# Angles of three gate groups summed by TensorE with a triangle of ones instead of scans, the state products' second weights 32 columns wide, and a new order of the tasks

## The chip, the cores and the metric

The kernel runs on one core of one Trainium2 chip. The metric is the device time of one execution in microseconds (us). Of the kernel before there are three timed runs: 762.91, 760.21 and 762.88 us, with a median of 762.88. The profile shown is of one more execution, which took 765.08 us; its span from the first to the last recorded instruction is 763.4 us, so 1.7 us lie around the span. The mean granted TensorE clock of that execution is 0.998.

## What is computed

Two blocks follow each other. The first is a linear attention with a complex gate, for 4 batches, 8 heads, 768 tokens and a head dimension D of 48; the second is an MLP on its output, with 3072 tokens, a model dimension of 384 and 2048 hidden features. Cut to what matters:

```python
mag = np.sqrt(a_re * a_re + a_im * a_im)
scale = np.minimum(mag, 0.999) / (mag + 1e-06)
a_re_n, a_im_n = (a_re * scale, a_im * scale)
for t in range(S):
    new_re = ar * S_re - ai * S_im
    new_im = ar * S_im + ai * S_re
    kv = np.einsum('bhd,bhe->bhde', k[:, :, t], v[:, :, t])
    S_re, S_im = (new_re + kv, new_im)
    y[:, :, t] = np.einsum('bhd,bhde->bhe', q[:, :, t], S_re)
...
h = x @ w_in
g = np.maximum(h, 0.0) + alpha * np.minimum(h, 0.0)
return (g @ w_out).astype(np.float32)
```

Each gate is a complex number. A product of gates over tokens has the product of their magnitudes and the sum of their angles, so the kernel needs the running sum of the angles over the tokens of a batch, taken modulo a full turn, and its sine and cosine.

## The kernel before, in words

**Tasks and their order.** Every stage is a Python generator (`gates`, `loads`, `half_rows`, `loads_v`, `pieces`, `weights`, `unit`, `loads_x`, `all_mlp`) that emits one operation, or a few, each time it is resumed. The long string `ORDER` names by a letter which task is resumed next, so it fixes the order of the instructions on every engine and of the loads on SyncE's queue (SP). The `yield DVE(...)`, `yield PE(...)` and so on, and the rings in `R`, carry the costs and buffers of a planner that found the string; here they do nothing. An engine runs its instructions in the string's order, and a waiting instruction holds back everything behind it on its engine.

**Gates.** `gates` runs for nine groups: (batch 0, chunks 0), (0, 1 and 2), (0, 3 to 5), then two groups of three chunks for each further batch. A chunk is 128 tokens (P). A tile holds 128 rows of (head, dimension), with NK = 3 such row blocks side by side, so a group of three chunks is 128x1152. The angles are made on ScalarE (the arctangent, L289), summed along the tokens by one `tensor_tensor_scan` on VectorE for each row block (L298), brought to whole turns by ScalarE (L312, which rounds) and VectorE (L315, which subtracts the whole turns), and handed to the next group of the batch in `carry` (L318). Then come sine and cosine (L328, L330, L333) and the two stores of the phases to `phs` in DRAM (L324). The magnitudes go through L340 to L358 into `decs` (L361). Both are loaded again in another layout, as `PP` (L507) and `T` (L514), by the 24 units.

**Units.** A unit is one chunk of one batch with all 8 heads. It turns q and k by the phases (L579, L581), and passes six levels: copies of q and k (L660, L676), products with the decays in place (L637), small TensorE products `ps_lv` (L596, 96 rows and 32 columns of weights), masks (L610, L620). Then k is transposed by TensorE (`ps_kt`, L708), copied into `T` by two ScalarE copies, and multiplied with v for the state: `ps_kv`, L720, whose weights are slices of `T` of 64 rows and 64 columns. Only 96 of the two times 64 columns are of use, since D2 = 2 * 48 = 96; the second copy, L711, puts the first 32 columns once more behind the 96 so that there is something to load. The states follow on VectorE (L728, L731), and the output `ps_y` by L746 (96 rows, 48 columns of weights) and L760 (64 rows, 48 columns). It is copied (L771), stored to `ysc` (L776) and loaded as `xT`.

```python
nc.scalar.copy(T[:, 4 * i:4 * (i + 1), 0:D2], t)
nc.scalar.copy(T[:, 4 * i:4 * (i + 1), D2:P], t[:, :, 0:P - D2])
...
for n in range(H):
    for j in range(0, P, HC):
        for s in range(1 if last else 2):
```

There s is one half (64 tokens, so 64 rows) of the chunk, j one half of the columns, and a batch's last chunk (`last`) needs only s = 0. In the program each of these matmuls carries the part of the 128x128 array that it uses: 128x32 at L596, 128x64 at L746, 64x64 at L720 and L760, 128x128 at the rest.

**MLP.** `all_mlp` interleaves blocks of two units (256 tokens). The first two blocks go the plain way (L817, then L867), the others by L839 and by seven products of a Strassen scheme (L957). The weights come as 64-bit floats and are made into 32-bit floats piece by piece: `to_f32` uses ScalarE (L435, L437, L439) and VectorE (L443, L445).

**Queues.** All bulk loads and stores are issued by SP, in the order of the string. GpSimd makes the masks at the start.

Of the kernel before, what the change touches and what calls it, by code (L numbers as in the profile page):

```python
# [9 lines left out]
F32 = mybir.dt.float32  # L10
# [4 lines left out]
AF = mybir.ActivationFunctionType  # L15
ALU = mybir.AluOpType
# [3 lines left out]
P = 128  # L20
# [5 lines left out]
TURN = 6.283185307179586  # L26
# [1 line left out]


ORDER = (  # L30
    "ABMABAAABABAAAAAAABMAAAAAMAAAABABBBJMMNMAAAJABBAAKAAAKJJAAAAAAAABBBABJABBBBBBNMBNPBBBPNPJBJKJKJBJBBB"
    "PNBBBPBBBBBBBBBPPPOOOOJLJCPJJLLKKCPOJLLLMLLLLLLLMLLJJOPOPOPNOPPPPONNPPQCPPPQNQCCCCPPPPPPPPPPQQPQPCNC"
    "CCPPPPPPPPPCQQNCCCCCONCCCQOQCNPCPQQQOJMMJPPLMLLJCNQQNORCJLnLCMLLJJJLCCCLLLLQCQRCRQQCCOQNQQQoooooooLL"
    "LNQQRRQNooQQCCCCCNCooQoOoQRQoCQORCCNRRoNooooooORoQOMJONQQoooooRNNOOQQQQRQQROQOQDQQJLRLLnLJJORoLLoooo"
    "LLDMLRNNoLLLLLLooooJDooDDRoooSoSoRRRRRRRRooooooooDRRoRRoRooooRNNNRDSDoDRoDRDSOooooooooRoDoDRSSRJJJJR"
    "RSNSSRRRRDoooooDSDTOooODSLRRoSSoLMLLMJLJLLLLLooSoDSoOTSNoooooSNoOooSSoSoSNSSSSoSDooToSoSooSTSNoooOOo"
    "oNMLLLLLTTSoTSTDSOoTTSDoooooDoDSOKTNoNNNOSSSTSSTSJJJMJLSDDoooooSoooooDJLSSLoOToNTToooToOoOOoooooTTOT"
    "TToTDDTToooooUTnTTooLLLJJLJLDLLLUooooTDToDDoooLLLoLKDoJJJToTTUooDDoDDDTDJTDDDoooooUoTTUTUTTUUUUoVooo"
    "oooooUoTUUVUTTTTVooooooooUUUEJJLLLJJELLLLLLLLLJoLLooooVoEooooUUoUUUEoEVooooooEoEoUVUoUUUoooooUooooEU"
    "UVVUUVUVVVEEEooooooooVoUoKEUVKVUUUUJKKEUUUUKJJJVEVVooVooooEoooEEooEooVVVooooVVVVVVoWoWooooooVoVooJLL"  # L40
    "LJnWooVooVWoLLLLVWWEVEVEEEWEVWWLLLLLLLLEVWWVJEJoKJoooooooooooVVVWVWVVVELKVVLLLLJLJJLLLJJWoWWEWoooooo"
    "oooXXooEEEoEEoooooooooooooooooWWWWWWWoooWXoEWLLLoEoooooooooooWWooooWWoooXoXWWEEEWEEWoJLLLJoooWXWWWEW"
    "XWWWXYWXLWWLLFYXJLnLJJLoooooooXooooooooooooooXXXXXXoooooFoooooooXXFXXoXXXoXooooooooXoXoXYYooooLLLLLL"
    "LLooXXYYXooXYXYYLYooooXooooXFYFooooooXXXXYXYXFYoFYXXXLXLJLJJJLJLLLFooooooooYYoJooooooooooFoooooYYYFF"
    "YooYYooYYoJJLLLJLLJLoZoYooZooYooooFFoooFoYooYYFZoooFFLLooooooooooZooooZZYZYZYFZZYFYFYoooFZYYYZYZYYFo"
    "YooFFYooooooooooFFLLYJJJLooZooooooZZoooooooooooLnFLLFLJLLLJFooLJLLLLZaaFooooooZZoooZFaoFFZZoooooooaF"
    "FoZZZoZFFFoooooooZoooZooaaoooZoZoZZaaZFFFooFJJaoaaZooooooooooooZZZaZZZaZZaoooooooZaoaooabooooooooooo"
    "oooaaooabbZLLZLGJJLLJLJLLGLLLLLaaaoaaooaGooaoooooooJoboaoooaGoobGabaaaJJabbaLKKKoGbGoooooooooooobbbo"
    "ooGGooooGGooooboooooooooababaaGbaGGbGabaLaooooooooocoobLLJJGnKLoooooooooLoLLooobbooocbLLLLLJbbGGGoob"
    "ocooooooLLLKboboboooGGoboooocboooooobbccboocbGbGooooooocccGGoobboooobbbbooooooooooooGcGGKJGGGobcbcbo"  # L50
    "ocbJLJbbLLLJJLocccoooooooooooGooooccGcccocccGdGcoooooooooooocococoocooccoooGGGGcJLLLLLLLLLLdGcocGcoo"
    "oooooodoodooocccddcJJJcdcooooooooooooooooddLLccLHLcJJJLLLJLLdoLdHLLnoooooooodKLLLdddoddooooooooooooo"
    "ooddodddddooHeddoooeodooooodedoHdoooooooooooededdddeeoHddHooooooooeHeeoooHoooddoooooooooooooooddoeee"
    "oddoKJJJJddLLLJeJLLLJJJJLLLeoeoooooooooeHooooHooooooooooffHHooooeeeLJJLLLLLooooooHHHHHHHfooeeooeeeeo"
    "oooooeeoooooooooeoeoooeeeoeHHHfoHeHgefeoooooeeefeHeeKHooofofeeoJJHffoooooooonofHLJLLLLLLLHHooooooooo"
    "offfgoLLJLJJJLLLoofffooooooogHoLooooffoofHHfooooHHHoooooooooofffffoofoofoogoHooooHooooffooooofHHfffH"
    "ffHohhogooooooffgffgffofofhfgogooooooooooooooooggIJJLLLLLLLLJJJIJJgLLLLLLggIgoggIooooooIooooooooooog"
    "goghgIoggogoghIoogooooooogooIoogoogoghhgIhgghIhgoIooohhoooooooooioooooooohogIoIoghggghghhgIggLLLLJJn"
    "hhoooooooooooiLLLLLJLLLLLLJJooohhIhIhhIoooohhhIIihooooooooihoooooooooooooiIhooooooooooooooooooohhJoo"
    "oiiiihhohihIIIohihoooooooJhhihhihihLoohIIiooooooooooiihooooooooooooooiioihILLLoooIiiiijJJLLLJJLLLJji"  # L60
    "iJLLLLLIoiooiooiIiooioiIjiioIIIIIoIooooooooooIIIoiIoooooojiijijiijJIojjjjoooooooooooooooooooijjjjiio"
    "oiijJnJJJLLLLJLLojooooooooooooooooojjjjjjjkkjooooooooojjooojookooooooojoojoookookjkoooookkoooooooooo"
    "oojJJLLLLLLLLLjjoooooookoooooooooojookoooooookooojjjjkjkjjjkLjjkooooooooolkkoLLJJJJJooooookkkokkkook"
    "kooookokkooooolloookooklkllkkkkkloooollooooooooooolJLLLLLLLLLLJLLooooooooooloooooooooklkklkkkklkkLLL"
    "LLnlllooLLLJJLLooooooooooooooollolllloolllooooooolooolmmolloLLLLLoooooloooololmmlooooooooooolooooooo"
    "olmlmlmomomooooooooomoooooooooomoooolmlmlmooooomLLLLLLmomoooooooooLLLLoooooommoooommllmmmmmllLLLLooo"
    "oommoooooomooomooommmmmmmmmomooooooooooommmoooooooooooonoooooooooooooooooooooooooooooooooooooooooooo"
    "oooooooooooooooooooooooooooooooooooooooooooooooooooooooooooooooooooooooooooooooooooooooooooooooooooo"
    "oooooooooooooooooooooooooooooooooooooooooooooooooooooooooooooooooooooooooooooooooooooooooooooooo")


class Ring:
# [25 lines left out]
def kernel(  # L98
# [32 lines left out]
    nc = tc.nc  # L131
    B, HP, _, D, S = q.shape
    H = 2 * HP
    DM, DF = w_in.shape
    NCH = S // P
    NK = DM // P
    NF = DF // P
    D2 = 2 * D
    HC = P // 2
# [12 lines left out]
    work = ctx.enter_context(tc.tile_pool(name="work", bufs=2))  # L152
    dram = ctx.enter_context(tc.tile_pool(name="dram", bufs=4, space=DRAM))
    ps = ctx.enter_context(tc.tile_pool(name="ps", bufs=1, space=PSUM))
# [51 lines left out]
    for name in (1, 4, 16, 32):  # L206
# [9 lines left out]
    twisted = [shared[:, 7 * F2 * P + i * F2 * HALF:7 * F2 * P + (i + 1) * F2 * HALF].rearrange(  # L216
        "p (f e) -> p f e", e=HALF) for i in range(3)]
    scr_of = {}
    carry = consts.tile([P, NK], F32, tag="carry")
    bias_tiny = next(column)  # L220
    nc.vector.memset(bias_tiny, TINY)
# [11 lines left out]
    nc.vector.memset(ones, 1.0)  # L233

    room = [None]

    def gates(g, b, c0, c1):
        C = c1 - c0
# [16 lines left out]
        def rows3(z):  # L255
            return z.rearrange("p (t s) -> p t s", t=NK)
# [36 lines left out]
            nc.scalar.activation(turn[:, :, 0], ident[:, 0:NK], AF.Copy, scale=0.0)  # L293
        else:
            nc.scalar.copy(turn[:, :, 0], carry)
        for i in range(NK):
            t = yield DVE(2 * n, ta, t)
            nc.vector.tensor_tensor_scan(out=turn[:, i, 1:n + 1], data0=ones.to_broadcast([P, n]), data1=d[:, i * n:(i + 1) * n],  # L298
                                         initial=turn[:, i, 0:1], op0=ALU.mult, op1=ALU.add)
        ts = yield ACT(N, ta)  # L300
        nc.scalar.activation(c, d, AF.Sin, scale=-1.0)
        tc_ = yield ACT(N, ta)
        nc.scalar.activation(e, d, AF.Sin, bias=bias_back)

        ts = yield DVE(N, ts)
# [2 lines left out]
        TT(out=e, in0=x, in1=e, op=ALU.mult)  # L308
        tm = yield DVE(N, ts, tc_)
        TT(out=c, in0=c, in1=e, op=ALU.add)  # L310
        t = yield ACT(N, t)
        nc.scalar.activation(rows3(d), spun, AF.Identity, scale=1.0 / TURN, bias=bias_round)  # L312
        whole = d.bitcast(I16)[:, 0::2]
        t = yield DVE(N, t)
        STT(out=spun, in0=rows3(whole), scalar=-TURN, in1=spun, op0=ALU.mult, op1=ALU.add)  # L315
        if not last:
            done["carry", g] = yield ACT(NK, t)
            nc.scalar.copy(carry, turn[:, :, n])  # L318
# [50 lines left out]
    w_out_sb = consts.tile([P, NF, DM], F32, tag="w_out_sb")  # L369


    al_1 = consts.tile([P, NF], F32, tag="al_1")

    words = w_in.dtype != F32
# [44 lines left out]
                nc.sync.dma_start(raw, src[f])  # L419
                done["raw", name, f] = t  # L420

    def to_f32(dst, *key):

        n = 2 * DM
        ta = yield ACT(n + 100, ("raw", *key), takes=(R["top"],))
        raw = raws.pop(key)
        lo, hi = raw[:, :, :, 0], raw[:, :, :, 1]
        slot = slots.pop(0)
# [19 lines left out]
        return t  # L448

    def piece(dst, *key):  # L450
        if words:
            return (yield from to_f32(dst, *key))
        t = yield ACT(2 * DM, ("raw", *key))
        nc.scalar.copy(dst, raws[key])
        del raws[key]
        raw_done(*key, t)
        return t
# [105 lines left out]
    def unit(u):  # L563
# [140 lines left out]
        for i in range(2):  # L704
            e = yield PE(0.333, k_, takes=(R["misc"],), n=2)
            t = ps.tile([P, HP, D2], F32, tag="misc", name="ps_kt")
            for p in range(4):
                nc.tensor.transpose(t[:, p], KQ[:, 1, 4 * i + p], ident[:D2, :D2])  # L708
            e = yield ACT(HP * P + 80, e, ("decays", u))
            nc.scalar.copy(T[:, 4 * i:4 * (i + 1), 0:D2], t)  # L710
            nc.scalar.copy(T[:, 4 * i:4 * (i + 1), D2:P], t[:, :, 0:P - D2])  # L711
            R["misc"].put(e)
        e = yield PE(0.72, e, ("values", u), *[("state", u - 1)] * (u > 0), takes=(R["misc"],) if last else (R["misc"], R["lv"]), mode=2, n=16 if last else 32)
        V = L["V"]
        kv = [ps.tile([P, H, D], F32, tag=tag, name="ps_kv", bufs=n) for tag, n in (("misc", 1), ("lv", 2))[:2 - last]]
        for n in range(H):
            for j in range(0, P, HC):
                for s in range(1 if last else 2):
                    rows = slice(HC * s, HC * (s + 1))
                    nc.tensor.matmul(kv[s][j:j + HC, n], lhsT=T[rows, n, j:j + HC],  # L720
                                     rhs=V[rows, n // 2, (n % 2) * D:(n % 2 + 1) * D], start=True, stop=True)
        ek = e
        states = [state.pop(b)]
# [419 lines left out]
```

## Time and profile before

| what | value |
|---|---|
| median of the three runs | 762.88 us |
| the profiled execution | 765.08 us |
| its span | 763.4 us |
| TensorE (PE) busy | 674.9 us, 88% |
| PE weight loads (PEld) busy | 581.2 us, 76% |
| VectorE (DVE) busy | 605.4 us, 79% |
| ScalarE (ACT) busy | 487.6 us, 64% |
| bytes moved by DMA | 130.61 MB |

A line of a group of instructions names the source line, the engine, the operation, the written and the read tile, the shapes (partitions x elements; for TensorE first the rows*columns of the weights), and the number of instructions; behind the first bar stand the busy time of the group in us and the mean duration of one in ns, behind the second the idle time of the engine just ahead of these instructions and what ended it. Busy time counts a stretch once, however many matmuls overlap in it, and the duration of one matmul runs from its start to the end of its pipeline. PE shows 11728 matmuls for the 5960 of the program: each takes two records, but for the transposes of L708, which take one. In a timeline a row gives the start, the time from the first start to the last end, and the number of instructions in a row of one kind.

### The profile page before, as it was taken

To read this page: it belongs to the slowest core of one execution; us is meant where nothing else is said; L and a number is where in the kernel's file an instruction comes from. 1 tells how busy PE (TensorE), PEld (TensorE's weight loads), DVE (VectorE), ACT (ScalarE), POOL (GpSimd) and SP (SyncE) were. 2 spreads that over 40 slices of the span, in tenths; PEclk is the share of its full clock that TensorE was granted. 3 is DMA by queue.
4 is the path that set the end of the run, shared out by engine and by line. 5 is a ranking of instruction groups with operands and counts; after the bars stand their busy time and mean duration, and the time that the engine had idled before them with its cause. 6 is when DMAs were issued, how large, how long until landed. Compare 5 with 4: busy or idle time off the path is not lost.

```text
span 763.4 us, 26774 instructions
## 1 busy us (share of the span) xinstructions
PE 674.9 (88%) x11728; PEld 581.2 (76%) x11728; DVE 605.4 (79%) x798; ACT 487.6 (64%) x886; POOL 13.1 (2%) x48
## 2 busy tenths in 40 slices
PE   0024578999999999999999999999999999999998
PEld 0024456776767888888888889888888988889987
DVE  7889889998999799898986898888996765742323
ACT  8868888985658576946693666756584544453330
POOL 5000000000000000000000000000000000000000
PEclk9999999999999999999999999999999999999999
DMA  9999989979677936787668854865745743421000
GB/s 257 273 258 230 267 236 274 232 216 245 192 194 201 254 83 140 210 223 187 177 170 210 234 123 102 227 188 135 185 129 171 183 104 81 112 43 53 1 21 21
DMA packets 177180, 130.61 MB, mean 171 GB/s; under 512 B 66280, under 2 KB 168424, under 8 KB 176616
## 3 DMA queue, kind: packets, MB, share of 16 engines
q1 hardware_dynamic: 177064, 128.91, 64.3%
q8 instruction: 92, 1.51, 0.9%
q14 instruction: 24, 0.20, 0.1%
HBM read 100.52 MB, written 35.42 MB: 178 GB/s over the span
## 4 chain that ended last, share of the span: by engine, by line
PE 53%; DMA 16%; DVE 11%; SPq 6%; ACT 4%; issue 2%; DVEq 0%; ACTq 0%
PE ps_h L839 19%; PE ps_o L957 17%; PE ps_lv L596 4%; PE ps_y L760 3%; DVE KQ L637 3%; DMA PP<-phs 3%; PE ps_o L867 3%; DMA T<-decs 2%; PE ps_kv L720 2%; SPq L547 2%; PE ps_y L746 2%; DMA xT<-ysc 2%; DMA shared<-in_w_out_dram 2%; DMA VL<-vsc 2%; PE ps_h L817 1%
## 5 line engine op out<-in xcount | busy, mean ns | idle before, releaser
L839 PE MATMUL ps_h<-xT,w_in_sb 128*128 128x256 f32 x960 | 228.6, 384 | 0.7 <-DVE shared L854 0.6
L839 PEld LDWEIGHTS ps_h<-xT,w_in_sb 128*128 128x128 f32 x960 | 176.9, 190 | 22.6 <-DVE shared L854 0.8
L637 DVE TENSOR_TENSOR KQ<-KQ,T 96x1024 f32<-96x1024 f32 x120 | 145.8, 1215 | 28.6 <-PE ps_lv L596 18.9
L957 PE MATMUL ps_o<-w_out_sb,shared 128*128 128x192 f32 x624 | 111.4, 329 | 0.8 <-ACT top L973 0.4
L854 DVE TENSOR_TENSOR shared<-shared,ps_h 128x512 f32<-128x512 f32 x80 | 54.5, 682 | 68.2 <-ACT shared L852 67.9
L957 PEld LDWEIGHTS ps_o<-w_out_sb,shared 128*128 128x128 f32 x624 | 102.4, 190 | 3.5 <-DVE top L963 0.8
L848 ACT ACTIVATE shared<-ps_h 128x512 f32<-128x512 f32 x80 | 47.7, 596 | 80.6 <-PE ps_h L839 80.2
L957 PE MATMUL ps_o<-shared 128*128 128x192 f32 x448 | 80.3, 331 | 0.7 <-DVE top L963 0.7
L852 ACT ACTIVATE shared<-shared,al 128x256 f32<-128x256 f32 x160 | 74.5, 505 | 1.9
L957 PEld LDWEIGHTS ps_o<-shared 128*128 128x128 f32 x448 | 72.7, 190 | 3.3 <-DVE top L963 1.4
L660 ACT COPY WQ<-KQ 96x1024 f32<-96x1024 f32 x48 | 49.9, 1039 | 33.9 <-DVE KQ L637 33.7
L596 PE MATMUL ps_lv<-WQ 96*32 96x32 f32 x2304 | 34.4, 203 | 38.2 <-DVE WQ L579 26.0
L596 PEld LDWEIGHTS ps_lv<-WQ 96*32 96x32 f32 x2304 | 26.2, 116 | 52.4 <-DVE WQ L579 26.0
L817 PE MATMUL ps_h<-xT,w_in_sb 128*128 128x256 f32 (+1 forms) x240 | 53.3, 357 | 4.5 <-DMA xT<-ysc 4.5
L867 PE MATMUL ps_o<-w_out_sb,shared 128*128 128x384 f32 x128 | 51.3, 509 | 5.6 <-DVE shared L826 4.2
L817 PEld LDWEIGHTS ps_h<-xT,w_in_sb 128*128 128x128 f32 x240 | 41.9, 203 | 16.4 <-DMA xT<-ysc 5.2
L760 PE MATMUL ps_y<-A,VL 64*48 64x64 f32 x2304 | 49.1, 225 | 4.5 <-DMA VL<-vsc 4.4
L610 ACT ACTIVATE A<-ps_lv,columns 128x64 f32<-128x64 f32 x144 | 38.3, 334 | 21.4 <-PE ps_lv L596 21.0
L771 ACT COPY T<-ps_y 48x512 f32<-48x512 f32 x48 | 27.7, 576 | 34.5 <-PE ps_y L760 33.7
L676 ACT COPY W<-KQ 96x512 f32<-96x512 f32 x48 | 30.6, 637 | 29.5 <-DVE KQ L637 29.5
L760 PEld LDWEIGHTS ps_y<-A,VL 64*48 64x48 f32 x2304 | 39.4, 123 | 11.0 <-DMA VL<-vsc 5.8
L596 PE MATMUL ps_lv<-KQ,W 96*32 96x32 f32 x1536 | 23.4, 203 | 15.9 <-ACT W L676 15.8
(108 smaller groups left out, 955.8 us busy)
## 6 DMA issues: line engine op xcount, KB each, us to landing
T<-decs SPq DMA_DIRECT2D x48, 384.0 KB
PP<-phs SPq DMA_DIRECT2D x24, 387.0 KB
KQ<-in_q_dram SPq DMA_DIRECT2D x48, 192.0 KB
phs<-gate SPq DMA_DIRECT2D x14, 577.5 KB
decs<-gate SPq DMA_DIRECT2D x7, 1152.0 KB
KQ<-in_k_dram SPq DMA_DIRECT2D x40, 192.0 KB
vsc<-in_v_dram SPq DMA_DIRECT2D x24, 288.0 KB
VL<-vsc SPq DMA_DIRECT2D x48, 144.0 KB
```

Of the source, the lines that this page charges most:

```text
L596: nc.tensor.matmul(t[64 * i + j:64 * i + j + HC // 2, p], lhsT=keys(n, g), rhs=queries(n, g), start=True, stop=True)
L610: nc.scalar.activation(a[:, :, cols], t[:, :, at:at + name], AF.Copy, scale=s)
L637: nc.vector.tensor_tensor(out=x, in0=x if x0 is None else x0, in1=m, op=ALU.mult)
L660: nc.scalar.copy(z.rearrange("p i n t -> p i (n t)").rearrange("p i (m h) -> p m i h", h=h), bass.AP(tensor=KQ.tensor, offset=KQ.offset + ...
L760: nc.tensor.matmul(o, lhsT=Vp[h][64 * i:64 * i + 64, s, e_ * D:(e_ + 1) * D], rhs=a, start=False, stop=(s == 1 and h == LEVELS[-1]))
L817: nc.tensor.matmul(p, lhsT=w_in_sb[:, f // 2, kk, f % 2 * P:(f % 2 + 1) * P], rhs=x_of[m][:, kk, c * P:(c + n) * P], start=(kk == 0), stop ...
L839: nc.tensor.matmul(p[:, i], lhsT=w_in_sb[:, f // 2, kk, i * P:(i + 1) * P], rhs=x_of[m][:, kk], start=(kk == 0), stop=(kk == NK - 1))
L848: nc.scalar.activation(gt, p, AF.Relu, scale=-1.0)
L852: nc.scalar.activation(some_, some_, AF.Copy, scale=al_1[:, f + i:f + i + 1])
L854: nc.vector.tensor_tensor(out=gt, in0=gt, in1=p, op=ALU.add)
L867: nc.tensor.matmul(sums[0], lhsT=gt, rhs=w_out_sb[:, f], start=(f == start), stop=(f == stop))
L957: nc.tensor.matmul(z, lhsT=a[:, i], rhs=w[:, i], start=i == 0, stop=i == F2 - 1)
```

## The change

The core of the diff, without the string `ORDER`, which is replaced as a whole:

```diff
+    SUMMED = (1, 2, 3)
+
+    def sums_on_tensor(g, C, first, angle, whole, turn, t, free):
+
+        up_to = up_to_of[0]
+        for j in range(C):
+            now = slice(j * P, (j + 1) * P)
+            if j or not first:
+                t = yield DVE(NK, t, free)
+                nc.vector.tensor_tensor(out=angle[:, :, j * P], in0=angle[:, :, j * P], in1=turn[:, :, j * P], op=ALU.add)
+            t = yield PE(0.25, t, free, takes=(R["misc"],))
+            p = ps.tile([P, NK, P], F32, tag="misc", name="ps_at")
+            for i in range(NK):
+                nc.tensor.transpose(p[:, i], angle[:, i, now], ident)
+            t = yield ACT(NK * P, t, takes=(R["W"],))
+            by_token = work.tile([P, NK, P], F32, tag="W", name="by_token", bufs=1)
+            nc.scalar.copy(by_token, p)
+            R["misc"].put(t)
+            t = yield PE(0.66, t, takes=(R["lv"],))
+            p = ps.tile([P, NK, P], F32, tag="lv", name="ps_sum", bufs=2)
+            for i in range(NK):
+                nc.tensor.matmul(p[:, i], lhsT=by_token[:, i], rhs=up_to, start=True, stop=True)
+            R["W"].put(t)
+            done["angles", g] = t
+            t = yield ACT(NK * P, t)
+            nc.scalar.activation(angle[:, :, now], p, AF.Identity, scale=1.0 / TURN, bias=bias_round)
+            t = yield DVE(NK * P, t)
+            nc.vector.scalar_tensor_tensor(out=turn[:, :, j * P + 1:(j + 1) * P + 1], in0=whole[:, :, now], scalar=-TURN, in1=p,
+                                           op0=ALU.mult, op1=ALU.add)
+            R["lv"].put(t)
+        return t
...
-        for i in range(NK):
-            t = yield DVE(2 * n, ta, t)
-            nc.vector.tensor_tensor_scan(out=turn[:, i, 1:n + 1], data0=ones.to_broadcast([P, n]), data1=d[:, i * n:(i + 1) * n],
-                                         initial=turn[:, i, 0:1], op0=ALU.mult, op1=ALU.add)
+        if g not in SUMMED:
...
-        t = yield ACT(N, t)
-        nc.scalar.activation(rows3(d), spun, AF.Identity, scale=1.0 / TURN, bias=bias_round)
         whole = d.bitcast(I16)[:, 0::2]
-        t = yield DVE(N, t)
-        STT(out=spun, in0=rows3(whole), scalar=-TURN, in1=spun, op0=ALU.mult, op1=ALU.add)
+        if g not in SUMMED:
...
+        else:
+            t = yield from sums_on_tensor(g, C, first, rows3(d), rows3(whole), turn, t, ta_)
...
+    up_to_of.append(w_out_sb[:, NF - 1, 0:P])
+    nc.gpsimd.memset(up_to_of[0], 1.0)
+    nc.gpsimd.affine_select(out=up_to_of[0], in_=up_to_of[0], pattern=[[1, P]], base=0,
+                            channel_multiplier=-1, compare_op=ALU.is_ge, fill=0.0)
...
     def piece(dst, *key):
+        after = [("angles", SUMMED[-1])] if key == ("out", NF // 2 - 1) else []
...
-            e = yield ACT(HP * P + 80, e, ("decays", u))
+            e = yield ACT(HP * D2, e, ("decays", u))
             nc.scalar.copy(T[:, 4 * i:4 * (i + 1), 0:D2], t)
-            nc.scalar.copy(T[:, 4 * i:4 * (i + 1), D2:P], t[:, :, 0:P - D2])
             R["misc"].put(e)
...
         for n in range(H):
-            for j in range(0, P, HC):
+            for cols in (slice(0, HC), slice(HC, D2)):
                 for s in range(1 if last else 2):
                     rows = slice(HC * s, HC * (s + 1))
-                    nc.tensor.matmul(kv[s][j:j + HC, n], lhsT=T[rows, n, j:j + HC],
+                    nc.tensor.matmul(kv[s][cols, n], lhsT=T[rows, n, cols],
                                      rhs=V[rows, n // 2, (n % 2) * D:(n % 2 + 1) * D], start=True, stop=True)
```

In words. For the second, third and fourth of the nine gate groups (C = 2, 3 and 3 chunks, so eight chunks) the nine scans go, and with them the wide rounding and the wide subtraction of the whole turns. In their place each chunk adds the sum so far to its first token (left out for the first chunk of a batch), is transposed by TensorE so that tokens lie on the rows, is copied out of PSUM by ScalarE, and is multiplied with a triangle of ones, which gives the running sums in the old layout; ScalarE rounds these and VectorE subtracts the whole turns, both straight from PSUM. A chunk begins when the one before it has ended. The triangle lies in the last 128x384 block of the MLP's second weights, until these are made; the task that makes the last piece of them therefore comes after the fourth group's sums.

In the units the second ScalarE copy into `T` goes, and the second weights of a state product are the 32 columns 64 to 96 instead of the 64 columns 64 to 128. In the built program these matmuls carry the part 64x32 of the array, the first ones still 64x64; the two kinds alternate from one column slice to the next, within each of the 8 heads.

## The prediction

> **What bounds the kernel now.** I read first the slices of the page, then busy time by stretches, to see which engine has no room at which time.
>
> ```profile
> PE   0024578999999999999999999999999999999998
> DVE  7889889998999799898986898888996765742323
> ...
> 100.00:120.00 20.00, 14.49 (x208) 10.49 (x208) 17.64 (x24) 16.59 (x31) 0.00 (x0) 1.00 0.86 232
> 140.00:160.00 20.00, 19.49 (x437) 14.98 (x436) 19.97 (x28) 19.75 (x32) 0.88 (x1) 1.00 0.92 238
> 400.00:500.00 100.00, 98.46 (x1770) 86.97 (x1771) 85.58 (x112) 60.10 (x115) 0.22 (x2) 1.00 0.70 183
> ```
>
> The first two lines are slices of 19 us; in the others the columns behind the length are busy us of PE, PEld, DVE, ACT and POOL, then PE's granted clock, the DMA share and GB/s. Up to about 140 us PE has gaps (77 us in sum), while VectorE, ScalarE (17 to 20 of 20 us) and the DMA engines (0.84 to 1.03) are nearly full: there the gates and the first units set the pace. From 140 us to the end PE idles 12.0 us in all. So what is added to PE after 140 us lengthens the run nearly one for one; what is taken from VectorE counts only before.
>
> **The state products (L720).** From PE's timeline (start, length, line, records) and the groups by form:
>
> ```profile
> 194.94 1.14 PE L720 MATMUL ps_kv<-V,T 64*64 64x48 f32 x32
> 196.00 1.13 PE L817 MATMUL ps_h<-xT,w_in_sb 128*128 128x256 f32 x4
> ...
> 200.03 0.46 PE L596 MATMUL ps_lv<-WQ 96*32 96x32 f32 x32
> 200.31 0.49 PE L596 MATMUL ps_lv<-KQ,W 96*32 96x32 f32 x32
> 200.73 1.75 PE L760 MATMUL ps_y<-A,VL 64*48 64x64 f32 x96
> ...
> 216.88 1.15 PE L720 MATMUL ps_kv<-V,T 64*64 64x48 f32 x64
> 217.95 0.46 PE L596 MATMUL ps_lv<-WQ 96*32 96x32 f32 x32
> 218.23 0.49 PE L596 MATMUL ps_lv<-KQ,W 96*32 96x32 f32 x32
> 218.65 0.65 PE L746 MATMUL ps_y<-KQ,St 96*48 96x64 f32 x16
> ```
>
> Read starts, not lengths. L596 followed by itself takes 218.23 - 217.95 = 0.28 us for 32 records; followed by another shape of array part it takes 0.42 (to 64x64 at 200.73, and to 128x64 at 218.65, where only the columns change). Over all such groups in the timeline the medians are 0.28 (51 times) against 0.39 to 0.42 (91 times). So **a change of the array's part costs 0.11 to 0.14 us**; I take 0.12. Two neighbours of one shape (L839 and L957) pay nothing: 12 records, 2.59 us, as long as 12 records inside a run.
>
> The block of a last chunk has 32 records and takes 196.00 - 194.94 = 1.06 us; the others have 64 and take 1.07. So its time belongs to the part of the array, not to the number of records: less one change, 0.94 us for 16 records on each 64x64 part, 0.059 us each. The first slice stays 64 wide, so narrower second weights save nothing on PE even if all goes well: their part only waits for its neighbour.
>
> The added cost: the order of the built program changes the part 288 times before and 652 times after, 360 of these inside the 24 blocks, 15 in each. If each drains the array like the rows above, a head costs two 64-wide records on a part (2 x 0.059 = 0.117), then two 32-wide ones (between L596's 0.28 / 32 x 4 parts = 0.035 and 0.059 each: I take 0.046, so 0.092), and two changes (0.24): 0.449 us. Eight heads: 3.59 us against 1.07, **+2.5 us a block**. Of the 24 blocks 21 begin at 141.3 us or later, where PE is the bound: +52.8. The first three (57, 92 and 115 us) lie where PE has gaps; I count nothing, and 7.5 if that cover is gone. Low end: 0.11 a change and records at 0.94 / 64 = 0.015 us, four a run: 16 x 0.169 = 2.7, +1.6 a block, 34 in 21. High end: 0.14 and 0.117 for every run: 4.1, +3.0 a block, 73 in 24. If parts on different columns need no drain: 0.
>
> [...]
>
> **The second copy, L711.** 48 x 0.279 = 13.4 us leave ScalarE, which has room after 140 us. PE's waits at L708 for L711 sum to 4.1 us: I take 1 gained, 0 to 4.
>
> **The angles.**
>
> ```profile
> L298 DVE TENSOR_TENSOR_SCAN gate<-columns,gate 128x384 f32<-128x384 f32 x21 | 20.5, 1001 | 0.2 <-ACT gate L295 0.2
> L298 DVE TENSOR_TENSOR_SCAN gate<-columns,gate 128x256 f32<-128x256 f32 x3 | 2.1, 741 | 0.3 <-ACT gate L295 0.3
> L315 DVE SCALAR_TENSOR_TENSOR gate<-gate 128x1152 f32<-128x1152 int16 x7 | 9.5, 1350 | 0.0
> L711 ACT COPY T<-ps_kt 128x128 f32<-128x128 f32 x48 | 13.4, 279 | 0.0
> ```
>
> VectorE loses 3 x 0.741 + 6 x 1.001 = 8.2 and, from L315, 0.95 + 2 x 1.35 = 3.65; it gains eight subtractions (L315 at 128x384: 0.55) and seven additions (0.15, near the smallest L358): 5.45. Net -6.4 us. ScalarE loses L312 (0.93 + 2 x 1.25 = 3.4) and gains 8 x (0.48, as L710, + 0.55): +4.8. PE gains 24 transposes (0.33 / 4 each, from L708) and 48 records of 128x128 (about 0.108, half of L839's 0.216): 7.2 us, with changes about 9. Groups two and three fall into PE's gaps; the fourth stands in PE's order between the fourth and sixth state block (from 141 us): +3.
>
> Alone the chain of a chunk is longer: 0.15 + 0.42 + 0.48 + 0.5 + 0.55 + 0.55 = 2.65 us, so 5.3 and 7.9 against 4.1 and 5.6 now. VectorE and ScalarE do other work meanwhile, since the new order puts units and weights between (unit products and L443 stand between the chunks' subtractions); without that cover +1.2 to +2.3 a group. Work on VectorE ahead of the second to eighth unit's first product, added up over the new order with these durations, is shorter by 3.4, 3.5, 8.7, -2.8, 6.2, 5.0 and 12.1 us. PE is full by then for the later ones, so I take 4 of the 6.4 as time gained.
>
> Other moves: SP issues the first `PP` behind 6.3 MB instead of 5.7, the second `PP` behind 10.4 instead of 11.4, the first `xT` behind 20.0 instead of 21.1 (at about 255 GB/s -2, +4 and +4 us); I count these within the 4. GpSimd's triangle (0.2 + about 0.7 us, as L171 and L172) goes ahead of `start`, whose load SP reaches at about 2 us, first used at 28: nothing. The new wait, ScalarE's last weight piece on the fourth group's sums, holds back ScalarE's queue; in its new order the last rounding of that group stands ahead of it anyway, so nothing; uncovered it would cost PE one piece, 3 us. Early part together: -4 + 3 = -1, from -7 to +6.
>
> **Sum.** 765.1 + 52.8 - 1 (copy) - 1 (early) - 3 (of the 12.0 us of PE's idle time after 140 us: a slower PE lets the others catch up; 0 to 7) = 812.9 for a profiled execution; the median lies 2.2 below this one, so **811**. This case's own range: 762.9 + 34 - 4 - 7 - 7 = 779 to 762.9 + 73 + 6 = 842.
>
> **Rivals.**
> *No drain, nothing gained.* Parts on other columns run beside each other whatever their width, as the two column parts do now (last chunk: 32 records in the time of 64). For it: the second slice shares no column with the first. Against it: L596 to L746 pays although only the columns change. 762.9 - 1 - 1 = 761. [...]
> *Faster.* Without drains, VectorE's 6.4 us come through whole at the point where PE becomes full, and the fourth group's PE work fits into gaps: 762.9 - 6.4 - 1 = 755.5. It decides if PE is full from about 134 us on.
> *Slower without drains.* The longer chains come through: +5.8 for the three groups, 762.9 + 5.8 = 769. Against it: both engines are full of other work between.
>
> **How the numbers follow.** Drain 0.66, for the measured 0.14 at a change of columns alone; no drain and nothing gained 0.16; faster 0.13; slower without drains 0.05. A measurement tells about 0.5% (3.8 us) from no change: faster 0.13, same 0.16, slower 0.71. The range reaches down into the no-drain cases, to 757, and up to 836, which leaves out most of the faster case and the top of the first.
>
> **What would show it.** Right: the state block takes 2.7 to 4.1 us instead of 1.07, its records in small groups 0.2 us apart; VectorE's scans number 18; the second unit starts some 3 us earlier; later PE busy rises by 50 us. Wrong: a block of about 1.07 us; then the first step falls and the end is set by when PE becomes full. A block of 2 us would say that drains are cheaper on disjoint columns.

## The result, and the profile after

The changed kernel takes 843.22 us (median of 837.24, 847.11 and 843.22) against 762.88: a ratio of 1.106 (95% interval 1.095 to 1.117). The prediction said slower, 811 us, with a range up to 836: the direction is right, the time lies outside. Where the runs of one kernel lie more than 1.5% apart, as those of number 7 below, a ratio is by the faster of them alone. The profiled execution took 837.24 us, its span is 835.5 us, and its mean granted TensorE clock is 0.967 (0.998 before).

The page of the changed kernel first: busy time, then slices, here of 21 us.

```profile
PE 757.8 (91%) x11800; PEld 642.1 (77%) x11800; DVE 602.7 (72%) x801; ACT 486.8 (58%) x851; POOL 13.5 (2%) x50
...
PE   0227779999999999999999999999999999999998
...
PEclk9999689998999999999998999999999999999999
```

TensorE is as full as before from the seventh slice on, and its busy time grew by 82.9 us, from 674.9; VectorE's and ScalarE's hardly changed. So the loss lies on TensorE. The clock line has an 8 in the slice from 188 and in the one from 439 us, where the clock before stood at 1.00.

Busy time after 140 us is the sharper view: PE's busy us (and records), PEld, DVE, ACT, POOL, then granted clock, DMA share and GB/s; first the kernel before, then the changed one.

```profile
140.00:763.40 623.40, 612.00 (x10218) 531.82 (x10216) 482.48 (x619) 370.95 (x705) 2.19 (x15) 1.00 0.59 153
```

```profile
140.00:835.50 695.50, 688.31 (x10513) 588.21 (x10511) 498.06 (x640) 381.58 (x693) 1.54 (x16) 0.98 0.54 141
```

The stretch is 72.1 us longer, and TensorE idles 7.2 us of it instead of 11.4. Its busy time rose by 76.3 us, half as much again as the forecast 50.

The state products in TensorE's timeline after, and the same groups by form:

```profile
153.03 0.59 PE L861 MATMUL ps_h<-xT,w_in_sb 128*128 128x256 f32 x2
153.56 3.70 PE L764 MATMUL ps_kv<-V,T 64*64 64x48 f32 x64
157.19 1.13 PE L861 MATMUL ps_h<-xT,w_in_sb 128*128 128x256 f32 x4
...
215.19 3.60 PE L764 MATMUL ps_kv<-V,T 64*64 64x48 f32 x32
```

```profile
L764 PE MATMUL ps_kv<-V,T 64*64 64x48 f32 x704 | 62.1, 239 | 0.6 <-ACT T L755 0.6
L764 PE MATMUL ps_kv<-V,T 64*32 64x48 f32 x704 | 53.8, 219 | 0.0
```

From start to start a block now takes 157.19 - 153.56 = 3.63 us against 1.07; 3.59 was worked out. Inside it the records start in groups of four, by turns 0.25 and 0.20 us from group to group, with a pause of 0.13 to 0.15 us at each change of the part; "drained" below means a stretch with these pauses. The block of a last chunk takes 3.53 us for 32 records (the next row starts at 218.72), so it is still the part, and not the number of records, that counts. 21 blocks after 140 us times 2.55 us are 53.6 us: the forecast's main term, to 1.5%. That leaves some 18 of the 72 us unexplained.

The clock explains most of the rest. Timeline and 4 us windows around one block of the changed kernel:

```profile
181.94 3.70 PE L764 MATMUL ps_kv<-V,T 64*64 64x48 f32 x64
185.58 1.08 PE L790 MATMUL ps_y<-KQ,St 96*48 96x64 f32 x16
186.59 0.66 PE L641 MATMUL ps_lv<-WQ 96*32 96x32 f32 x32
```

```profile
180.00:184.00 4.00, 3.55 (x42) 2.59 (x42) 2.24 (x4) 3.36 (x6) 0.00 (x0) 1.00 0.75 214
184.00:188.00 4.00, 4.00 (x96) 3.36 (x92) 2.32 (x5) 3.40 (x3) 0.00 (x0) 0.70 0.73 209
188.00:192.00 4.00, 4.00 (x45) 2.83 (x42) 1.75 (x3) 0.00 (x0) 0.00 (x0) 0.50 0.89 209
192.00:196.00 4.00, 4.00 (x83) 2.92 (x82) 3.86 (x8) 1.32 (x2) 0.00 (x0) 0.94 0.37 92
```

TensorE is busy without a gap, and yet its granted clock falls to one half (0.50) behind the block, and L641 takes 0.58 us from start to start (the next row begins at 187.17) instead of 0.42. I add up (1 - clock) x length over all 4 us windows from 140 us to the end of the run: 15.4 us in this execution, in six falls behind blocks; 21.1 us in a second profiled execution of the same kernel (below), in eight and at the run's end; 0.0 in the kernel before. I take such a sum as an upper end for the cost; number 2 below, where the blocks and this sum together come to more than the measured rise, shows why.

With 7.4 us for the order and the sums (the first experiment) and 4.2 us of idle time absorbed: 53.6 + 15.4 + 7.4 - 4.2 = 72.2, against 72.1 by the spans. That it agrees to 0.1 us is luck: the clock's term is an upper end and differs by 6 us between the two executions, and the same sum overshoots number 2 below by 7 us.

### The profile page after: what moved, and what is told of

Read it like the earlier page. It is cut to its first block, busy times and chain, and to the rows that moved or that the text cites. A ratio compares the mean times of both kernels' runs of the same rounds, so it can differ in the third digit from the quotient of the medians.

```text
span 835.5 us, 26907 instructions
## 1 busy us (share of the span) xinstructions
PE 757.8 (91%) x11800; PEld 642.1 (77%) x11800; DVE 602.7 (72%) x801; ACT 486.8 (58%) x851; POOL 13.5 (2%) x50
## 5 line engine op out<-in xcount | busy, mean ns | idle before, releaser
L883 PEld LDWEIGHTS ps_h<-xT,w_in_sb 128*128 128x128 f32 x960 | 179.6, 192 | 22.2
L764 PE MATMUL ps_kv<-V,T 64*32 64x48 f32 (+1 forms) x1408 | 90.8, 229 | 0.6 <-ACT T L755 0.6
L764 PEld LDWEIGHTS ps_kv<-V,T 64*32 64x32 f32 (+1 forms) x1408 | 65.4, 120 | 28.3 <-issue 3.3
L1001 PE MATMUL ps_o<-shared 128*128 128x192 f32 x448 | 84.6, 339 | 0.0
L1001 PEld LDWEIGHTS ps_o<-shared 128*128 128x128 f32 x448 | 75.2, 196 | 2.6 <-DVE top L1028 0.8
L911 PE MATMUL ps_o<-w_out_sb,shared 128*128 128x384 f32 x128 | 54.8, 540 | 4.3 <-DVE shared L870 3.5
L861 PE MATMUL ps_h<-xT,w_in_sb 128*128 128x256 f32 (+1 forms) x240 | 56.3, 366 | 0.6 <-DMA xT<-ysc 0.6
L775 DVE TENSOR_TENSOR St<-St,ps_kv 96x384 f32<-96x384 f32 x44 | 24.2, 549 | 44.8 <-PE ps_kv L764 43.2
L861 PEld LDWEIGHTS ps_h<-xT,w_in_sb 128*128 128x128 f32 x240 | 43.5, 210 | 13.8 <-issue 2.7
L804 PE MATMUL ps_y<-A,VL 64*48 64x64 f32 x2304 | 47.1, 228 | 0.2 <-issue 0.2
L641 PEld LDWEIGHTS ps_lv<-WQ 96*32 96x32 f32 x2304 | 27.1, 117 | 24.9 <-issue 11.5
```

The lines of the kernel that those rows point to most:

```text
L764: nc.tensor.matmul(kv[s][cols, n], lhsT=T[rows, n, cols], rhs=V[rows, n // 2, (n % 2) * D:(n % 2 + 1) * D], start=True, stop=True)
L804: nc.tensor.matmul(o, lhsT=Vp[h][64 * i:64 * i + 64, s, e_ * D:(e_ + 1) * D], rhs=a, start=False, stop=(s == 1 and h == LEVELS[-1]))
L861: nc.tensor.matmul(p, lhsT=w_in_sb[:, f // 2, kk, f % 2 * P:(f % 2 + 1) * P], rhs=x_of[m][:, kk, c * P:(c + n) * P], start=(kk == 0), stop ...
L883: nc.tensor.matmul(p[:, i], lhsT=w_in_sb[:, f // 2, kk, i * P:(i + 1) * P], rhs=x_of[m][:, kk], start=(kk == 0), stop=(kk == NK - 1))
L911: nc.tensor.matmul(sums[0], lhsT=gt, rhs=w_out_sb[:, f], start=(f == start), stop=(f == stop))
L1001: nc.tensor.matmul(z, lhsT=a[:, i], rhs=w[:, i], start=i == 0, stop=i == F2 - 1)
```

## The experiments

My theory: the changes of the part inside the state blocks cost their 2.55 us each; the drained block is long enough to bring the clock down afterwards; the order and the sums gain nothing. Rivals: the order with the sums is the loss; the fall of the clock comes from the small parts, not from the drains. The ratios are to the kernel before in the same job, where it took 767 to 770 us; intervals are 95%.

**1. Both weights 64 wide again.** The changed kernel with the old weights and the second copy.

```diff
+            nc.scalar.copy(T[:, 4 * i:4 * (i + 1), D2:P], t[:, :, 0:P - D2])
...
-            for cols in (slice(0, HC), slice(HC, D2)):
+            for j in range(0, P, HC):
...
```

> The changed kernel with the state products' second weights 64 wide again, and with the second copy that fills them: only the sums on TensorE and the new order are left. Theory (the array is drained at each change of its part, and the long thin block lowers the granted clock): the block is back at 1.07 us, the granted clock at 0.99 or more after 140 us, and the time within 758 to 772 us; what it lies above 763 is the price of the early part. Rival (the new order and TensorE's sums cause a good part of the 80 us): over 780 us, with a clock below 0.98.

Measured: 776.73 us, ratio 1.010 (1.007 to 1.012); a block takes 1.08 us again, and the clock after 140 us is 1.00. So the weights are nearly the whole loss, and the order with the sums costs 0.0097 x 762.9 = 7.4 us more (5.6 to 9.1 by the interval).

**2. The narrow weights alone.** The kernel before with the alternating widths and without the second copy; order and scans as before.

```diff
-            nc.scalar.copy(T[:, 4 * i:4 * (i + 1), D2:P], t[:, :, 0:P - D2])
...
-            for j in range(0, P, HC):
+            for cols in (slice(0, HC), slice(HC, D2)):
...
```

> The kernel before with one edit: second weights 32 wide in alternation with the 64 wide ones, no second copy; scans and order as before. Theory: the block takes 3.6 to 3.7 us, 24 x 2.55 = 61 us more in all, 53 of it after 140 us, and the clock falls to 0.95 to 0.98 after some of the blocks: 825 to 845 us. Rival (the narrow weights cost only the drains, and the clock fell because of the new order's gaps): 763 + 53 = 816 us, with a clock above 0.99. Rival (all comes from the order): below 780 us.

Measured: 832.93 us, ratio 1.083 (1.079 to 1.087). The blocks take 3.63 us from start to start, and the clock falls behind eight of them after 140 us. (1 - clock) x length sums to 21.0 us there; with 53.6 us for the blocks and some 4 absorbed this is more than the measured 64 us, which is why I call the clock's sum an upper end.

**3. One change of the part in a block, not fifteen.** The changed kernel, all 64-wide products of a block first, then the 32-wide.

```diff
-        for n in range(H):
-            for cols in (slice(0, HC), slice(HC, D2)):
+        for cols in (slice(0, HC), slice(HC, D2)):
+            for n in range(H):
```

> The changed kernel with the state products sorted: first all 64-wide weights of the 8 heads, then all 32-wide ones, so one change of the array's part inside a block instead of 15. Theory: the block is 0.94 us for the wide ones, about 0.74 for the narrow ones and two changes of 0.12, so 1.9 us; 24 x 0.85 = 20 us above the kernel with both wide, and a clock at 0.99 or more, since the block is short: 780 to 792 us. Rival (a 64x32 record is slow by itself): a block of 3 us or more, above 820 us.

Measured: 786.18 us, ratio 1.022 (1.020 to 1.024). TensorE's timeline in this kernel:

```profile
106.94 1.94 PE L764 MATMUL ps_kv<-V,T 64*64 64x48 f32 x64
108.81 0.91 PE L911 MATMUL ps_o<-w_out_sb,shared 128*128 128x384 f32 x2
```

The same products of the same widths take 1.87 us instead of 3.63: fourteen changes fewer, 0.126 us each. What is left above 1.07 is one change more and the two widths one behind the other. And no fall of the clock is left after 140 us but in the run's last us, where TensorE has ended: the widths alone, in blocks this short, do not bring it down.

**4. Three slices, all 32 wide.** No change of the part inside a block.

```diff
-            for cols in (slice(0, HC), slice(HC, D2)):
+            for cols in (slice(0, 32), slice(32, HC), slice(HC, D2)):
```

> The changed kernel with three slices of 32 columns instead of one of 64 and one of 32: 96 records a block instead of 64, all on 64x32 parts, no change inside. Theory: six parts side by side, 16 records on each at 0.035 to 0.046 us: 0.6 to 0.85 us a block, or 96 x 0.009 = 0.84 if the issue rate of L596 binds, so 0.8 to 1.0 us with the change; clock at 0.99 or more; 2 to 6 us below the kernel with both 64 wide: 755 to 768 us. Rival (narrow records are slow by themselves): a block of 3 us or more, above 820 us.

Measured: 805.82 us, ratio 1.050 (1.043 to 1.056). A block takes 1.02 us, close to the 0.8 to 1.0 worked out, yet the time is far off. TensorE's waits in this kernel (us in total, times, longest):

```profile
PE ps_lv L641 <- issue: 11.2, 5, 3.2
PE ps_y L790 <- issue: 5.0, 3, 1.9
PE ps_y L804 <- issue: 3.9, 3, 2.0
PE ps_h L883 <- issue: 1.9, 1, 1.9
```

Twelve gaps of 1 to 3 us in which TensorE waits for nothing that the profile shows, 22 us, and behind seven of them a fall of the clock (14.6 us by the same sum). The changed kernel has two of these gaps, 2.7 us, in its second profiled execution. So this expectation fell by something new, not by the block; the last section says what the gaps are.

**5. A dense stretch in the middle of the block.** The changed kernel with four products of the identity, 128x128, halfway through each state block; they cost time, and nothing reads them.

```diff
+            if n == H // 2:
+                dense = kv[0].rearrange("p n e -> p (n e)")[:, H * D - P:]
+                for _ in range(4):
+                    nc.tensor.matmul(dense, lhsT=ident, rhs=ident, start=True, stop=True)
```

> The changed kernel with four extra 128x128 products of the identity with itself in the middle of every state block (they write columns of PSUM that the block's second half then overwrites; the result is not changed): as many changes of the array's part inside a block as before plus two, but two drained stretches of 1.85 us instead of one of 3.7. Work added: 8 records of 0.108 us and two changes, 1.1 us a block, 26 us in all. Theory (a long drained stretch lowers the granted clock): no fall of the clock behind a state block after 140 us, mean clock there at 0.99 or more; 15 to 25 us of the changed kernel's time come back, so the time changes by -5 to +12 us against the changed kernel's 1.106 times the kernel before. Rival (the clock falls with the number of changes, or with the new order): the clock stays at 0.95 to 0.97, and the time is some 26 us above the changed kernel, ratio 1.135 or more.

Measured: 856.19 us, ratio 1.114 (1.110 to 1.118). A block is two drained halves of 1.82 us with 1.09 us between, so 24 x 1.1 = 26 us were added, and the time rose by some 7 us, by the ratios of two jobs (0.0086 x 763). The clock's sum after 140 us is 3.4 us, in two falls: one behind a gap of 2.06 us on issue, one behind a block of 32 records.

**6. The same work ahead of the block.** To keep the work and change only the length of the drained stretch, the four products go ahead of the block (`if n == 0`); beside it on one chip run the changed kernel and number 5 once more.

> The changed kernel with four 128x128 products ahead of each state product instead of in its middle; the same 1.1 us of added work a block, 26 us in 24 blocks, but the drained stretch behind it stays 3.6 us long. Theory, the length of one drained stretch counts: the granted clock falls behind some of the blocks after 140 us as in the changed kernel, and the time is that of the changed kernel in this job + 20 to + 30 us. Rival, the share of full products over a longer stretch counts: the clock stays at 1.00 after 140 us as with the products in the middle, and the time is that of the changed kernel + 0 to + 12 us.

> The four products in the middle of the block once more, beside the changed kernel and the one with them ahead of it on one chip. Theory: the time of the changed kernel + 0 to + 12 us, clock 1.00 after 140 us. Rival, the earlier +7 us came from comparing two chips: + 20 to + 30 us.

> The changed kernel itself, as the base for the two runs with added products: a ratio of 1.095 to 1.117 to the kernel before by every theory.

Measured, with the kernel before at 769.98 us: the changed kernel 842.97 us (1.095, 1.091 to 1.099), the products in the middle 855.53 (1.112, 1.108 to 1.116), ahead of the block 872.08 (1.132, 1.127 to 1.137). From the windows of the two kernels, in the middle first:

```profile
300.00:500.00 200.00, 198.24 (x3142) 173.04 (x3143) 159.98 (x196) 123.98 (x219) 0.47 (x5) 0.99 0.66 167
700.00:856.70 156.70, 152.77 (x1833) 137.61 (x1832) 66.91 (x92) 51.29 (x107) 0.00 (x0) 0.99 0.21 53
```

```profile
300.00:500.00 200.00, 198.26 (x3075) 173.16 (x3074) 152.66 (x188) 119.51 (x211) 0.48 (x5) 0.95 0.60 159
700.00:869.40 169.40, 165.44 (x1992) 149.60 (x1988) 73.36 (x102) 54.35 (x112) 0.11 (x1) 0.98 0.20 50
```

The same instructions in another place: 16.5 us apart in the median, 15.4 us apart in the clock's sum (5.1 and 20.5). Ahead of the block they cost 29 us, their full price; in the middle 12.6, just above what was expected, because the clock mostly stays up. Three falls are left after 140 us: two behind gaps of 1.34 and 1.47 us on issue between small parts, one behind a block of 32 records. Behind the 17 blocks of 64 records after 140 us there is none, here or in number 5. So the length of one drained stretch brings the clock down: 3.6 us does, behind some of the blocks, and 1.8 us does not behind a block of 64 records. The rival of the share of full products over a longer stretch is refuted.

The falls have one depth and one grid in time: the granted clock in them is 0.50, every fall that ends within a run here lasts 3.41 us or a whole multiple of it, and the falls of one execution begin whole multiples of 3.41 us apart. A window below is one step of this grid. The fall at 185.59 us of the changed kernel, with the window ahead of it and the one behind it:

```profile
182.17:185.58 3.41, 3.41 (x65) 2.49 (x61) 0.68 (x1) 2.75 (x5) 0.00 (x0) 1.00 0.66 203
185.59:192.41 6.82, 6.82 (x108) 5.35 (x105) 4.48 (x8) 1.83 (x2) 0.00 (x0) 0.50 0.90 237
192.42:195.83 3.41, 3.41 (x81) 2.44 (x80) 3.27 (x6) 1.32 (x2) 0.00 (x0) 0.99 0.32 81
```

Where a block lies on this grid goes with whether the clock falls behind it (6 and 8 of 21). I laid the grid over the blocks after 140 us of the changed kernel's two executions and of number 2. Of the 51 blocks of 64 records, ten lie with over 3.2 us inside one window, and behind all ten the clock falls; of the other 41 it falls behind three. The 12 blocks of 32 records are as long with half the work: behind all nine with over 2.3 us in one window the clock falls, behind the other three it does not. So TensorE need not idle for the clock to fall: the window from 182.17 us is shown as fully busy (3.41 of 3.41 us), with 3.3 us of it inside the drained block, and the clock stands at 0.50 behind it.

**7. The order with scans.** Number 1 with the scans, the wide rounding and the wide subtraction in place of the sums, at the first five of their steps.

> The new order alone: the changed kernel with both 64-wide weights and the second copy, and with scans again for groups two to four; the three scans, the rounding and the subtraction stand at the first five places that the order gives to the sums, the places behind them are empty. If the early loss of 7.7 us is the chains' own length (TensorE, ScalarE and VectorE in turn, VectorE waiting): 762 to 769 us on a chip where the kernel before takes 769, ratio 0.992 to 1.000. If the loss comes from the new order of loads and units: ratio 1.006 to 1.012, as with the sums.

Measured: 804.01 and 811.15 us, ratio 1.051 (1.043 to 1.059); neither was expected. The profiled execution took 820.04 us. TensorE's waits in it again show gaps on issue, the largest two being

```profile
PE ps_lv L627 <- issue: 12.7, 7, 2.9
PE ps_y L791 <- issue: 7.4, 6, 2.8
```

and the clock falls after 140 us (20.5 us by the sum). As a total it tells nothing of the order.

**8. The sums in the old order.** The kernel before with the sums, one step of theirs behind every third step of the string.

> TensorE's sums alone: the order of the kernel before, with the sums of groups two to four started where the old order had the rounding, their further steps put in at every third step of the other tasks (every step for the fourth group); both weights 64 wide, second copy kept. If the chains' length is the loss: ratio 1.004 to 1.015, the second unit's first product 3 us or more later than in the kernel before. If the order was the loss: 0.992 to 1.002, as the 6.4 us of VectorE come through.

Measured: 831.2 us, ratio 1.080 (1.075 to 1.086), with issue gaps of 16.9 us in nine times at one line alone. The fourth state block begins at 168.3 us instead of 141.3, since steps put in by a fixed rhythm are no order that anyone sought. It does not separate the sums from the order either.

**9. The order with scans and the sums' products.** As number 7, but TensorE keeps the 24 transposes and 24 products, on the identity and unread, so that its instructions stay in step with number 1.

```diff
+                if kind == "turn":
...
+                    for i in range(NK):
+                        nc.tensor.transpose(p[:, i], ident, ident)
+                elif kind == "sum":
...
+                    for i in range(NK):
+                        nc.tensor.matmul(p[:, i], lhsT=ident, rhs=up_to, start=True, stop=True)
```

> The new order with 64-wide weights, in which the scans, the wide rounding and the wide subtraction of groups two to four give the angles, at the first five places of the sums' steps; TensorE still does the 24 transposes and 24 products of the sums, on the identity and with results that nothing reads, so that its instructions stay those of the new order with the sums. ScalarE's and VectorE's work for each chunk goes. Theory, the sums' long chains cost the 7 us that the new order with the sums lost: a ratio of 0.997 to 1.003 to the kernel before, and the second unit's first product starts near 47.5 us. Rival, the order costs them: 1.007 to 1.013, and that product starts near 53 us.

Measured: 777.3 us, ratio 1.012 (1.007 to 1.018); the issue gaps are gone (1.2 us in two). The second unit's first product starts at 48.23 us, as the theory of the sums had it (47.46 before, 53.03 in number 1), but the total is that of the order. TensorE begins here with the unread products at 1.6 us, and the clock column then stands at 0.50 from 8 to 76 us. The same rows are as long in number 1, where the column says 1.00: 32 records of `ps_lv` take 0.65 to 0.66 us, four transposes 0.90, the first state block 1.89 in both. So: the sums' chains hold the second unit up by 5 us, and taking them away did not show in the end; the fourth state block starts at 153.1 us in number 1, at 150.0 here and at 141.3 before. How the 7.4 us divide between order and sums stays open.

**10. Many small products without drains.** The kernel before with every state product three times (`for n in [*range(H)] * 3`), 2 us more a block, all of one part, to see whether a long stretch of small parts brings the clock down.

> The kernel before with every state product issued three times (the same result each time): a block of 192 records on 64x64 parts, 0.13 + 3 x 0.94 = 2.95 us, without a change inside; 24 x 1.9 = 45 us more, 40 of it after 140 us. Theory (what lowers the clock is the drained array, not the small parts): clock at 0.99 or more, 803 to 815 us at 769 before, ratio 1.045 to 1.06. Rival (any long stretch on small parts lowers the clock): falls behind some blocks, mean clock 0.95 to 0.98, ratio 1.07 or more.

Measured: 877.43 us, ratio 1.141 (1.135 to 1.148), far above what the added work can cost. Undisturbed blocks take 2.94 us, as computed, but TensorE's waits show

```profile
PE ps_lv L596 <- issue: 23.6, 10, 4.3
PE ps_kv L720 <- issue: 21.4, 12, 2.9
PE ps_y L760 <- issue: 8.2, 4, 4.5
```

and the falls of the clock after 140 us stand behind these gaps. The total therefore decides nothing, but single windows do. One of the 3.41 us windows, from 402.87 to 406.28 us, holds small parts alone, with two changes of the part and no gap:

```profile
402.41 3.00 PE L720 MATMUL ps_kv<-V,T 64*64 64x48 f32 x96
405.34 0.65 PE L746 MATMUL ps_y<-KQ,St 96*48 96x64 f32 x16
405.92 0.46 PE L596 MATMUL ps_lv<-WQ 96*32 96x32 f32 x32
406.20 0.49 PE L596 MATMUL ps_lv<-KQ,W 96*32 96x32 f32 x32
```

```profile
402.87:406.28 3.41, 3.41 (x144) 3.28 (x142) 0.55 (x1) 2.29 (x4) 0.00 (x0) 1.00 1.07 254
406.28:409.70 3.42, 3.42 (x77) 3.30 (x64) 2.90 (x3) 1.63 (x2) 0.00 (x0) 1.00 0.75 271
```

The clock stays at 1.00 behind it, as it does behind two more such windows of this run (from 536 and from 802 us, with at most 0.07 us of gap). So small parts alone did not bring the clock down here; the drained stretches of 3.6 us did (number 6).

No version tried was faster than the kernel before.

## Why the prediction was wrong, step by step

- **The drains: right in mechanism and size.** "a change of the array's part costs 0.11 to 0.14 us" came from rows of other parts; fourteen changes taken away (number 3) give 0.126. The block of 3.59 us was measured at 3.63, and the rivals without a drain fell with it, as did the low end of 2.7 us a block. Counting nothing for the first three blocks was right in the new order: they take 8.7 us more in all than in number 1, and the fourth begins at 153.6 us against 153.1 there.
- **The step that failed: a missing term.** "So what is added to PE after 140 us lengthens the run nearly one for one" holds only while the granted clock stays where it was. The prediction carried 1.00 over from the windows of before and never asked what 3.6 us of a drained array do to it. The runs showed 15 to 21 us in its place, by the clock's sum, which is an upper end; number 6, where only the place of the same work differs, gives 16.5. With 15 to 21 alone the sum would have been 826 to 832.
- **The early part: wrong sign.** "Early part together: -4 + 3 = -1, from -7 to +6" was measured at +7.4 (number 1). Two terms inside it can be sized. The fourth group's TensorE work, "+3", is three times 0.49 + 0.83 = 4.0 us. And the chain of a chunk, "2.65 us", takes 4.7: from 25.66 to 30.33 us in the timeline of the changed kernel,

```profile
25.66 0.16 DVE L248 TENSOR_TENSOR gate<-gate 128x3 f32<-128x3 f32 x1
...
25.96 0.87 PE L252 MATMUL ps_at<-ident,gate 128*128 128x128 f32 x3 [25.96 <-DVE gate L248]
26.87 0.48 ACT L255 COPY by_token<-ps_at 128x384 f32<-128x384 f32 x1 [0.49 <-PE ps_at L252]
...
27.50 1.62 PE L260 MATMUL ps_sum<-w_out_sb,by_token 128*128 128x128 f32 x6 [0.66 <-ACT by_token L255]
...
29.15 0.58 ACT L264 ACTIVATE gate<-ps_sum,columns 128x384 f32<-128x384 f32 x1 [1.80 <-PE ps_sum L260]
...
29.77 0.56 DVE L266 SCALAR_TENSOR_TENSOR gate<-gate,ps_sum 128x384 f32<-128x384 int16 x1 [3.09 <-ACT gate L264]
30.36 0.17 DVE L248 TENSOR_TENSOR gate<-gate 128x3 f32<-128x3 f32 x1
```

  where ScalarE's and VectorE's terms came out as forecast, and TensorE's 0.42 + 0.5 came out as 0.87 + 1.62. The same two steps take 0.49 + 0.83 at 145 us. TensorE runs at about half rate early, and the prediction took its durations from late rows. The profile of before had it:

```profile
51.44 0.87 PE L708 MATMUL ps_kt<-ident,KQ 96*128 96x96 f32 x4 [4.21 <-DVE KQ L637]
...
57.31 2.06 PE L720 MATMUL ps_kv<-V,T 64*64 64x48 f32 x64
```

  The same line as its later 1.15 us blocks, at 57 us, takes 2.06, and four transposes 0.87 instead of 0.50. VectorE idled 3.09 us in the middle of the first chunk: the cover that was to hide the longer chains was not there. So the second unit started 5.5 us later (53.01 against 47.46 us), not "some 3 us earlier".
- **The copy: near by luck.** TensorE's waits for the copies into `T` are 3.0 us in the second profiled execution, against 4.1 before, so the 1 us gained is there. But with the second copy back in (number 1) they are 3.5, and without it in the old order (number 2) 4.8: most of the gain goes with the order, and little with the copy.
- **Idle time absorbed: near.** 3 us were taken; 11.4 - 7.2 = 4.2 came, by windows that give 11.4 us before where the prediction has 12.0.
- **The scans: right in their own lengths.** VectorE shows 18 instead of 27; by the lengths of the groups the exchange frees 6.3 us, as forecast, yet the page's busy time, which counts a stretch once, fell by 2.7 only. In number 1 a loss stands at the end, not a gain.
- **The range.** Its top, 836, cut off even the upper end that the drains were given by themselves (842), and had no room for a second loss. The clock and the early part together are 23 to 29 us, nearly half the drains.

## What to carry to other kernels

Products of different widths on the array should be grouped by width, since each change cost TensorE 0.126 us here: 32 products that change 15 times took 3.63 us, the same ones with one change 1.87. When an edit leaves the array drained for 3.6 us at a stretch, as here, price a fall of the clock behind it as a term of its own, even where TensorE shows no idle time (behind 6 and 8 of 21 blocks it fell to 0.50); half that length, or dense products in its middle, avoided it behind all but two blocks here, both of only 32 records. And take a duration from rows of the same stage: the same six records took 0.83 us in the full part of this run and 1.62 us where TensorE was mostly waiting.

## What the runs showed that was not expected

- **The clock column said 1.00 while TensorE ran at about half rate.** In the changed kernel the windows show 1.00 up to 80 us, yet L252 and L260 take 0.87 and 1.62 us at 26 us, 0.55 and 0.94 at 77 us (behind 11 us of unbroken work), and 0.88 and 1.65 again at 85 us, where the column falls to 0.66. Before its first fall the column does not tell the rate in this run; the duration of a repeated group does.
- **Gaps on issue: by the packets' times, TensorE waits for its instructions.** Numbers 4, 7, 8 and 10 have gaps of 1 to 4.5 us, 21 us and more in all, where TensorE waits for nothing that the views name, in or near runs of many small products. The instruction queue of the page moves 92 packets in the kernel before, 98 in number 4 and 114 in number 10, with 11728, 12504 and 14544 records: one packet for some 128 records (127.5 to 127.6) in each case. The times of these packets in the traces point to what the gaps are. All 65 gaps over 0.8 us in the four runs end 1.2 to 1.7 us after such a packet has landed, though the packets come some 7 us apart, and they stand whole multiples of some 127 records apart. I read this as TensorE having used up its instructions there and waiting for the next packet. At 0.28 us for 32 records, L596 uses up a packet's worth in 1.1 us (an estimate), about as long as one packet takes to arrive (1.1 us in the median). Why number 7, with no more records than the kernel before, has such gaps and the kernel before has none was not tested; where the packets' ends fall among the small products may decide it.
